# A bias table indexed by distance, read in both directions by the product, in an attention-and-MLP kernel

## The chip, the cores and the metric

The kernel runs on one core of a Trainium2 chip. The metric is the device time of one execution in microseconds (us): 1127.53 us is the median of three runs of the kernel before (1126.89 to 1128.61).

## The reference

```
q, k, v: 4 batches x 8 heads x 576 positions x 64, float32
rel   = pos[:, None] - pos[None, :]
x     = log1p(|rel|) / log1p(max(pos_i, 1))              # 576 x 576
bias  = relu(x[..., None] @ w1 + b1) @ w2                # hidden 32 -> one value per head
attn  = softmax(q @ k.T / 8 + bias[head])                # rows over 576 keys
x     = (attn @ v), heads side by side                   # 2304 x 512
x     = (h - tanh(h)) @ w_out, with h = x @ w_in         # 512 -> 2048 -> 512
out   = (silu(x @ w_gate) * (x @ w_val)) @ w_out2        # 512 -> 1536 -> 512
```

All of it is in float32. The bias is the same for all batches and depends on q and k positions alone. Since log1p(max(pos_i, 1)) is positive, it is divided out behind the relu: relu(w1 * log1p|i-j| + b1 * psi_i) @ w2 / psi_i, with psi_i = log1p(max(i, 1)).

## The kernel before

There are four stages on one core: the bias rows are made, then 80 attention units run, then the first MLP, then the second. The MLPs take most of the span and are not touched.

**Bias rows.** 576 query positions make 36 groups G of 16 positions (`GEN_ORDER`: 32 to 35, 24 to 31, 16 to 23, 8 to 15, 0 to 7). A group has four blocks j of four positions; the partitions of a block are 4 positions x 32 hidden values. `bias_hidden(G)` makes for each block a tile `r` of 576 columns (one per key): a slice of the constant table `cst` (w1 * log1p of a distance, 1152 columns wide, multiplied by w1 on the chip in two pieces, L129), plus the block's own `b1p` column, clipped at zero. Blocks 0 to 2 are made on VectorE (DVE, L144), block 3 on ScalarE (ACT, L146). `bias_rows(G)` multiplies the four tiles by w2 on TensorE into one PSUM tile `bps` (128 partitions = 16 positions x 8 heads): four products of 512 columns (L166), four of 64 (L171), each run as two passes. ACT scales them by -1/psi (`nipsi`) into the row tile `bev` (L176), GpSimd (POOL) copies 64 columns to the row's front (L180), and SP stores the tile into a scratch tensor in DRAM (L182). The hidden tiles of the next group are issued ahead of the products of this one. There are four `r` buffers of two blocks each, and five `bev` buffers.

Keys stand in a permuted order: the first 512 as (t, p) for key 4p + t, and for the odd head of a pair the last 64 in front. That is why the product writes PSUM with `"p (t n) -> p n t"` and why the row has 64 columns twice.

**Order.** Each engine runs its instructions in the order in which the code emits them, without a scheduler. 33 groups are made ahead of the first attention unit (`GEN0`, `GEN_EACH`, `GEN_LATE`), with the loads and transposes of the first head pair between them; the last three groups (letter G in `FIRST_ORDER` and `STEP_ORDER`) lie in units 0 and 1. All DMAs are issued by SP, in order, on one hardware queue; a DMA that waits holds those behind it. A DMA's completion is counted on one of eight semaphores in turn (`DMAHW0` to `DMAHW7` where an order is shown), so a ninth DMA waits for the first of them to land. `due` says after how many further groups the finished 128-position table t is loaded back from the scratch (`bias_load`, tile `bt`, L193).

**Attention.** A unit is a head pair hp, a batch b and a span t of 128 queries (t = 4, 3, 2, 1, 0; 64 for t = 4). Scores are three products into PSUM (L315), DVE adds the bias and takes the row minimum (L330), ACT exponentiates (L341), POOL scales by the inverse sum (L359), TensorE transposes the probabilities (L381, L398), and the product with v (L436) follows. For the next pair TensorE transposes q and k (L243) into a PSUM tile of the pool that the scores use too; ACT copies them out (`kraw` L259, `qraw` L254 and L262), which frees that tile.

## Time and profile before

| what | us |
|---|---|
| median of three runs | 1127.53 (1126.89 to 1128.61) |
| the profiled execution | 1127.98 |
| its span (first to last instruction) | 1126.2 |
| around the span | 1.8 |
| TensorE (PE) busy | 1106.5 (98%) |
| VectorE (DVE) busy | 863.0 (77%) |
| ScalarE (ACT) busy | 765.2 (68%) |
| GpSimd (POOL) busy | 476.9 (42%) |

The chain of waits that ended last gives 84% of the span to PE, 7% to DVE and 3% to ACT. Shares over the whole span are means over four stages. The bias rows are made in the first 57.5 us; the rows further below look into that stretch. A busy PE is not PE at its peak: a product of 32 rows that runs beside three others is counted as busy for as long as any of them runs.

### The profile page before, as it was taken

Reading aid. Unit: us, or ns where it says so; the run is one execution under the profiler, and the core shown is the slowest. Engines: PE = TensorE matmul, PEld = TensorE weight load, DVE = VectorE, ACT = ScalarE, POOL = GpSimd, SP = SyncE. Lnnn points to the kernel's source line nnn. Section 1 sums busy time; section 2 is a strip of 40 time slices with the busy share of each in tenths; the row PEclk is TensorE's granted clock in tenths of the full one; section 3 lists DMA queues with packets and bytes.
Section 4 is the critical chain, followed back from the end, with each engine's and each line's share of the span. In section 5 each row is a group of like instructions: output and inputs, shape, how many; then the busy total and the mean of one; then the engine's idle time right before and its main releaser. Section 6 shows DMA issues by size and latency. Waiting matters only on the chain.

```text
span 1126.2 us, 21423 instructions
## 1 busy us (share of the span) xinstructions
PE 1106.5 (98%) x7772; PEld 925.4 (82%) x7772; DVE 863.0 (77%) x1691; ACT 765.2 (68%) x1530; POOL 476.9 (42%) x499
## 2 busy tenths in 40 slices
PE   7999999999999999999999999999999999999998
PEld 4577777777678888888888888999999999988887
DVE  7978999999698898989988888987667765774222
ACT  7989999999588888777777786546445445443112
POOL 3357777777445365344434344124323222351000
PEclk9999999999999999999999999999999999999999
DMA  5863535351111111101100010041422422763433
GB/s 190 293 173 103 154 81 168 83 172 53 49 57 56 38 51 43 57 19 57 57 19 29 29 38 1 21 138 58 139 89 72 140 85 79 251 204 103 158 94 112
DMA packets 93034, 107.47 MB, mean 95 GB/s; under 512 B 45312, under 2 KB 72064, under 8 KB 92928
## 3 DMA queue, kind: packets, MB, share of 16 engines
q1 hardware_dynamic: 92928, 106.10, 30.1%
q8 instruction: 61, 1.00, 0.4%
q14 instruction: 45, 0.37, 0.1%
HBM read 75.41 MB, written 30.67 MB: 94 GB/s over the span
## 4 chain that ended last, share of the span: by engine, by line
PE 84%; DVE 7%; ACT 3%; issue 1%; POOL 1%; DMA 1%; DVEq 0%; ACTq 0%; POOLq 0%
PE b L720 19%; PE h L720 17%; PE y L720 16%; PE o L720 13%; PE x L436 7%; PE s L315 6%; PE pTa L381 2%; DVE acc L62 1%; PE pTb L381 1%; ACT p L341 1%; DVE r L144 1%; PE pE L398 1%; DVE p L330 1%; DMA bias<-bev 1%; DVE w L62 1%
## 5 line engine op out<-in xcount | busy, mean ns | idle before, releaser
L720 PE MATMUL y<-gh,w 128*128 128x512 f32 (+1 forms) x748 | 197.3, 369 | 1.3 <-DVE xl L451 0.9
L720 PE MATMUL h<-xh,w 128*128 128x512 f32 (+1 forms) x640 | 191.0, 369 | 0.0
L720 PEld LDWEIGHTS y<-gh,w 128*128 128x128 f32 x748 | 133.9, 188 | 26.3 <-DVE xl L451 1.4
L720 PEld LDWEIGHTS h<-xh,w 128*128 128x128 f32 x640 | 116.9, 188 | 20.7 <-issue 0.5
L359 POOL TENSOR_SCALAR p<-p,r 128x576 f32<-128x576 f32 x144 | 109.6, 773 | 49.9 <-PE s L315 15.7
L720 PE MATMUL h<-xl,w 128*128 128x512 f32 (+1 forms) x320 | 117.8, 368 | 0.0
L341 ACT ACTIVATE p<-p,m 128x576 f32<-128x576 f32 x144 | 111.2, 775 | 1.2 <-DVE m L330 0.8
L330 DVE CUSTOM_DVE_ANT_0 p<-s,bt 128x576 f32<-128x576 f32 x144 | 103.6, 753 | 10.3 <-PE s L315 10.3
L720 PE MATMUL o<-w,xh 128*128 128x512 f32 x324 | 102.7, 389 | 0.0
L720 PE MATMUL b<-xh,w 128*128 128x384 f32 x360 | 101.3, 335 | 0.5 <-DVE sq L1209 0.5
L315 PEld LDWEIGHTS s<-k,q 64*128 64x128 f32 x768 | 57.6, 184 | 28.4 <-issue 17.6
L720 PE MATMUL y<-gl,w 128*128 128x512 f32 (+1 forms) x212 | 78.8, 372 | 1.8 <-POOL gl L62 1.8
L436 PE MATMUL x<-pt,vn 128*64 128x256 f32 (+1 forms) x512 | 79.1, 421 | 0.2 <-DVE xl L451 0.2
L315 PE MATMUL s<-k,q 64*128 64x288 f32 x768 | 73.1, 310 | 0.1
L62 POOL TENSOR_TENSOR gl<-g,gh 128x512 fp32r<-128x512 f32 (+1 forms) x27 | 33.2, 1230 | 90.4 <-issue 46.3
L720 PEld LDWEIGHTS o<-w,xh 128*128 128x128 f32 x324 | 60.8, 188 | 12.4
L720 PEld LDWEIGHTS h<-xl,w 128*128 128x128 f32 x320 | 60.4, 189 | 9.9
L720 PEld LDWEIGHTS b<-xh,w 128*128 128x128 f32 x360 | 65.9, 188 | 1.0 <-ACT acc21r L1102 0.8
L720 PE MATMUL b<-xl,w 128*128 128x384 f32 x180 | 60.2, 334 | 0.0
L829 ACT ACTIVATE sq<-h 128x512 f32<-128x512 f32 (+1 forms) x40 | 22.2, 556 | 50.7 <-PE h L720 50.7
L166 PE MATMUL bps<-r,cst 128*32 128x512 f32 x264 | 48.8, 634 | 7.6 <-DVE r L144 5.7
L720 PE MATMUL o<-w,xl 128*128 128x512 f32 x144 | 56.2, 390 | 0.0
(263 smaller groups left out, 2973.8 us busy)
## 6 DMA issues: line engine op xcount, KB each, us to landing
raw_out<-in_moe_w_out_dram SPq DMA_DIRECT2D x28, 512.0 KB, 3.5
bias<-bev SPq DMA_DIRECT2D x36, 320.0 KB, 3.4
bt<-bias SPq DMA_DIRECT2D x16, 576.0 KB, 5.1
s<-sq SPq DMA_DIRECT2D x24, 384.0 KB, 3.1
raw_in<-in_moe_w_in_dram SPq DMA_DIRECT2D x16, 512.0 KB, 4.0
xh<-s SPq DMA_DIRECT2D x15, 512.0 KB, 3.6
raw_gate<-in_moe_w_gate_dram SPq DMA_DIRECT2D x12, 512.0 KB, 3.8
raw_val<-in_moe_w_val_dram SPq DMA_DIRECT2D x12, 512.0 KB, 3.8
```

What stands on the lines that cost most here:

```text
L62: (engine or nc.gpsimd).tensor_tensor(out, a, b, ALU.subtract)
L144: nc.vector.tensor_scalar(r, src, b1, 0.0, ALU.add, ALU.max)
L166: nc.tensor.matmul(ps[0][32 * j:32 * j + 32].rearrange("p (t n) -> p n t", t=4), self.w2, R[j][:, 0:512].rearrange("p (n t) -> p n t", t=4 ...
L315: nc.tensor.matmul(self.st[u][j][:, e, 0:HALF], lhs, k[r, y, e * HALF:(e + 1) * HALF], start=n == 0, stop=n == 2,)
L330: nc.vector.tensor_tensor_reduce(out=p[:, n, :].rearrange("p (e f) -> p e f", e=2), in0=ps[n][:, :, 0:HALF], in1=bt[:, n, :].rearrange("p ...
L341: nc.scalar.activation(p[:, n, :], p[:, n, :], AF.Exp, bias=m[:, n:n + 1], scale=-1.0, accum_out=ls[:, n:n + 1],)
L359: nc.gpsimd.tensor_scalar(p[:, n, :], p[:, n, :], r[:, n:n + 1], 1.0, ALU.mult, ALU.mult)
L381: nc.tensor.transpose(half[h][:, 64 * m:64 * m + 64], p[r, j, k:k + 128], self.ident[r, r])
L398: self.nc.tensor.transpose(self.pt_end[:, at:at + 128], both, self.ident)
L436: nc.tensor.matmul(ps[r, 0:n], lhs, rhs, start=c == 0, stop=c == 4)
L720: nc.tensor.matmul(out, lhs[a], rhs[b], start=first and n == 0, stop=last and n == 2, skip_group_check=again)
L829: nc.scalar.activation(u, h, AF.Square)
```

## The change

The table now holds one column per distance: 576 columns instead of 1152, and column d is w1 * log1p(d) on all partitions. Seen from the last of a group's 16 positions, column c of its row lies at distance |16G + 15 - c|, and so one clipped tile serves both sides of the diagonal: the product reads it backwards (a step of -1) up to column 16G + 15, and forwards from there. The other 15 positions need the same row, shifted by one key each; the store does that. A group clips only as many columns as its largest distance needs, n = max(16G + 16, 576 - 16G), between 304 and 576. In ten groups (odd G from 9 to 27) DVE makes all four blocks, in the others three. The product of a group now has three segments of four (cut at column 16G + 15, where the direction turns, and at 512, where the PSUM bank ends), 591 columns in all instead of 576. The row tile has 591 columns; the store writes it into DRAM with a row pitch that is one element longer per position (`H * ROW + 1`), which shifts each position to its place. The POOL copy is gone. Keys stand in natural order; the odd head's bias is loaded back in two pieces, so a `bt` load is three DMAs instead of one (or two); v is loaded with two DMAs of 256-byte pieces; k is transposed like q, and `kraw` is copied in two instructions. The tables are loaded back six groups after they are due instead of two.

The table comes in with one DMA per 32 partitions, and in the last 32 partitions two columns are then overwritten by two small DMAs.

```diff
@@ -35,6 +35,8 @@
 C_W1 = C_NIPSI + NBLK
 C_B1, C_W2 = C_W1 + 1, C_W1 + 2
 NCONST = C_W2 + QG * H
+K_PSI, K_W1, K_B1, K_W2 = (c - TABW + S for c in (C_PSI, C_W1, C_B1, C_W2))
+ROW, BASE, WIDE = 640, 16, S + 15
 
 
 TORDER = (4, 3, 2, 1, 0)
@@ -102,18 +104,20 @@
         c = self.gen_p
         self.ident = self.const.tile([128, 128], F32, name="ident")
         make_identity(nc, self.ident)
-        self.cst = c.tile([128, NCONST], F32, name="cst")
-        nc.sync.dma_start(out=self.cst[:, TABW:NCONST], in_=self.packed[:, TABW:NCONST])
-        half = 640
-        nc.sync.dma_start(out=self.cst[:, 0:half], in_=self.packed[:, 0:half])
-        nc.sync.dma_start(out=self.cst[:, half:TABW], in_=self.packed[:, half:TABW])
-        b1c = self.cst[:, C_B1:C_B1 + 1]
+        self.cst = c.tile([128, S + NCONST - TABW], F32, name="cst")
+        nc.sync.dma_start(out=self.cst[:, S:], in_=self.packed[:, TABW:NCONST])
+        for g in range(QG):
+            at, x = slice(HID * g, HID * g + HID), S - 1 + g
+            nc.sync.dma_start(out=self.cst[at, 0:S], in_=self.packed[at, x:x + S])
+        for d in (S - 2, S - 1):
+            x = S - 1 + QG - 1 - d
+            nc.sync.dma_start(out=self.cst[at, d:d + 1], in_=self.packed[at, x:x + 1])
+        b1c = self.cst[:, K_B1:K_B1 + 1]
         self.b1p = c.tile([128, NBLK], F32, name="b1p")
-        nc.vector.tensor_scalar(self.b1p, self.cst[:, C_PSI:C_PSI + NBLK], b1c, None, ALU.mult)
-        self.table(self.cst[:, 0:half])
-        self.rest = self.cst[:, half:TABW]
-
-        self.w2 = self.cst[:, C_W2:NCONST]
+        nc.vector.tensor_scalar(self.b1p, self.cst[:, K_PSI:K_PSI + NBLK], b1c, None, ALU.mult)
+        t = self.cst[:, 0:S]
+        nc.vector.tensor_scalar(t, t, self.cst[:, K_W1:K_W1 + 1], None, ALU.mult)
+        self.w2 = self.cst[:, K_W2:]
         self.nipsi = c.tile([128, NG], F32, name="nipsi")
         rows = self.packed.rearrange("(g r) c -> g r c", g=QG)
         blocks = c.tile([128, NBLK], F32, name="blocks")
@@ -122,25 +126,19 @@
             nc.sync.dma_start(out=blocks[at, :], in_=rows[:, 0:H, C_NIPSI:C_NIPSI + NBLK])
             nc.gpsimd.tensor_copy(self.nipsi[at, :], blocks[at, j::4])
 
-        self.scratch = [self.dram.tile([n * H, S + 64], F32, name=f"bias_{t}") for t, (_, n) in enumerate(SPANS)]
-
-    def table(self, t):
-
-        self.nc.vector.tensor_scalar(t, t, self.cst[:, C_W1:C_W1 + 1], None, ALU.mult)
+        self.scratch = [self.dram.tile([n, H, ROW], F32, name=f"bias_{t}") for t, (_, n) in enumerate(SPANS)]
 
     def bias_hidden(self, G):
 
         nc = self.nc
         both = [self.gen_p.tile([128, 2, S], F32, tag="r", name=f"r_{G}_{i}", bufs=4) for i in range(2)]
         self.R[G] = []
-        if G == GEN_ORDER[1]:
-            self.table(self.rest)
         for j in range(4):
             blk = 4 * G + j
-            o = S - 1 - QG * blk
-            r = both[j // 2][:, j % 2, :]
-            src, b1 = self.cst[:, o:o + S], self.b1p[:, blk:blk + 1]
-            if j < 3:
+            n = max(16 * G + 16, S - 16 * G)
+            r = both[j // 2][:, j % 2, 0:n]
+            src, b1 = self.cst[:, 0:n], self.b1p[:, blk:blk + 1]
+            if j < 3 or 8 <= G < 28 and G % 2:
                 nc.vector.tensor_scalar(r, src, b1, 0.0, ALU.add, ALU.max)
             else:
                 nc.scalar.activation(r, src, AF.Relu, bias=b1, scale=1.0)
@@ -162,24 +160,27 @@
             both = None
             ps = [self.bank(tag, f"bps{tag}_{G}") for tag in ("cx" if n % 2 else "ab")]
 
-        for j in range(4):
-            nc.tensor.matmul(
-                ps[0][32 * j:32 * j + 32].rearrange("p (t n) -> p n t", t=4), self.w2,
-                R[j][:, 0:512].rearrange("p (n t) -> p n t", t=4), start=True, stop=True,
-            )
-        for j in range(4):
-            nc.tensor.matmul(ps[1][32 * j:32 * j + 32, 0:64], self.w2, R[j][:, 512:S], start=True, stop=True)
-        row = self.gen_p.tile([128, S + 64], F32, tag="bev", name=f"bev_{G}", bufs=BEV_BUFS)
-        out = row[:, 64:S + 64]
+        zero = 16 * G + 15
+        cuts = sorted({0, zero, 512, WIDE})
+        for a, b in zip(cuts, cuts[1:]):
+            d = a - zero
+            for j in range(4):
+                moving = R[j][:, d:d + b - a] if d >= 0 else R[j][:, -d:-d - (b - a):-1]
+                nc.tensor.matmul(
+                    ps[a // 512][32 * j:32 * j + 32, a % 512:a % 512 + b - a], self.w2, moving, start=True, stop=True,
+                )
+        row = self.gen_p.tile([128, WIDE], F32, tag="bev", name=f"bev_{G}", bufs=BEV_BUFS)
+        out = row
         ni = self.nipsi[:, G:G + 1]
         if both is not None:
-            nc.scalar.activation(out, both.rearrange("p e n -> p (e n)")[:, 0:S], AF.Copy, scale=ni)
+            nc.scalar.activation(out, both.rearrange("p e n -> p (e n)")[:, 0:WIDE], AF.Copy, scale=ni)
         else:
             nc.scalar.activation(out[:, 0:512], ps[0], AF.Copy, scale=ni)
-            nc.scalar.activation(out[:, 512:S], ps[1][:, 0:64], AF.Copy, scale=ni)
-        nc.gpsimd.tensor_copy(row[:, 0:64], row[:, S:S + 64])
+            nc.scalar.activation(out[:, 512:WIDE], ps[1][:, 0:WIDE - 512], AF.Copy, scale=ni)
         t, r0 = divmod(G, 8)
-        nc.sync.dma_start(out=self.scratch[t][128 * r0:128 * r0 + 128, :], in_=row)
+        to = self.scratch[t][16 * r0:16 * r0 + 16]
+        at = bass.AP(to.tensor, to.offset + BASE - 15, [[H * ROW + 1, 16], [ROW, H], [1, WIDE]])
+        nc.sync.dma_start(out=at, in_=row)
 
     def bias_load(self, hp, t):
         n = SPANS[t][1]
@@ -187,13 +188,14 @@
             [128, n // 64, S], F32, tag=f"bias{n}", name=f"bt_{hp}_{t}", bufs=4 if n == 128 else 1,
         )
 
-        x = 2 * hp * (S + 64) + 64
-        src = self.scratch[t].rearrange("(q h) k -> q (h k)", h=H)[:, x:x + 2 * S]
-        if n == 128:
-            self.nc.sync.dma_start(out=bt.rearrange("p j k -> p (j k)"), in_=src)
-        else:
-            for j in range(2):
-                self.nc.sync.dma_start(out=bt[64 * j:64 * j + 64, 0, :], in_=src[:, j * S:j * S + S])
+        for j in range(2):
+            src = self.scratch[t][:, 2 * hp + j, BASE:BASE + S]
+            to = bt[:, j] if n == 128 else bt[64 * j:64 * j + 64, 0]
+            if j == 0:
+                self.nc.sync.dma_start(out=to, in_=src)
+            else:
+                self.nc.sync.dma_start(out=to[:, 64:S], in_=src[:, 0:512])
+                self.nc.sync.dma_start(out=to[:, 0:64], in_=src[:, 512:S])
         self.bias_t[hp, t] = bt
 
 
@@ -203,9 +205,8 @@
         a = {"q": self.q, "k": self.k, "v": self.v}[nm][b, 2 * hp:2 * hp + 2]
         if nm == "v":
             t = self.nat.tile([128, 2, 4, D], F32, tag="v", name=f"vn_{hp}_{b}", bufs=2)
-            nc.sync.dma_start(
-                out=t.rearrange("p j t d -> p j (t d)"), in_=a[:, 0:512].rearrange("j (p t) d -> p j (t d)", t=4),
-            )
+            for j in range(2):
+                nc.sync.dma_start(out=t[:, j], in_=a[j, 0:512].rearrange("(t p) d -> p t d", t=4))
 
             end = self.vend[self.nbuf["v"] % 2]
             self.nbuf["v"] += 1
@@ -225,16 +226,16 @@
         t = self.nt[hp, b, "k"]
         nc.sync.dma_start(out=t[:, 0:4, 0, :], in_=by4(0, 0, 512))
         nc.sync.dma_start(out=t[0:64, 4, 0, :], in_=a[0, 512:576])
-        nc.sync.dma_start(out=t[0:64, 0, 1, :], in_=a[1, 512:576])
-        nc.sync.dma_start(out=t[64:128, 0:4, 1, :], in_=by4(1, 0, 256))
-        nc.sync.dma_start(out=t[0:64, 1:5, 1, :], in_=by4(1, 256, 512))
+        nc.sync.dma_start(out=t[0:16, 0:4, 1, :], in_=by4(1, 512, 576))
+        nc.sync.dma_start(out=t[16:128, 0:4, 1, :], in_=by4(1, 0, 448))
+        nc.sync.dma_start(out=t[0:64, 4, 1, :], in_=a[1, 448:512])
 
     def qk_transpose(self, hp, b, which):
 
         nc = self.nc
         nat = self.nt.pop((hp, b, which))
         ps = self.ps_s.tile([128, 2, 512], F32, tag="s", name=f"{which}T_{hp}_{b}")
-        parts = [(slice(t, 256, 4) if which == "q" else slice(64 * t, 64 * t + 64), nat[:, t, :, :]) for t in range(4)]
+        parts = [(slice(t, 256, 4), nat[:, t, :, :]) for t in range(4)]
         if which == "k":
             parts.append((slice(256, 320), nat[:, 4, :, :]))
         for to, a in parts:
@@ -255,12 +256,11 @@
                 self.qraw[:, 0:512].rearrange("p (h n) -> p h n", h=2), ps[:, :, 0:256], AF.Copy, scale=-0.125,
             )
             return
-        kraw = self.shared.tile([128, 640], F32, tag="one1", name=f"kraw_{hp}_{b}")
-        nc.scalar.copy(
-            kraw.rearrange("p (t h n) -> p t h n", t=5, h=2), ps[:, :, 0:320].rearrange("p h (t n) -> p t h n", t=5),
-        )
+        kraw = self.shared.tile([128, S], F32, tag="one1", name=f"kraw_{hp}_{b}")
+        nc.scalar.copy(kraw[:, 0:512].rearrange("p (h n) -> p h n", h=2), ps[:, :, 0:256])
+        nc.scalar.copy(kraw[:, 512:S], ps[:, 0, 256:320])
         nc.scalar.activation(self.qraw[:, 512:S], ps[:, 1, 256:320], AF.Copy, scale=-0.125)
-        self.raw_qk += [(hp, b, "q", self.qraw), (hp, b, "k", kraw[:, 0:S])]
+        self.raw_qk += [(hp, b, "q", self.qraw), (hp, b, "k", kraw)]
 
     def qk_high(self):
         nc = self.nc
@@ -487,7 +487,7 @@
                     self.bias_rows(G)
                     done = NG - len(gens)
                     if not any(x // 8 == G // 8 for x in gens):
-                        due.append((G // 8, done + 2))
+                        due.append((G // 8, done + 6))
                     if due and done >= due[0][1]:
                         self.bias_load(0, due.pop(0)[0])
                     if not gens:
```

On SP's queue the program now starts as follows (`cst` is the table, `blocks` the factors for the rows, `qn` and `kn` the first pair's q and k, `bev` the first row). Before:

```order
L106 DMA cst<-in_packed_dram 128x322
L108 DMA cst<-in_packed_dram 128x640
L109 DMA cst<-in_packed_dram 128x512
L122 DMA blocks<-in_packed_dram 32x1x144 x4
L222 DMA qn_0_136<-in_q_dram 128x4x64
L222 DMA qn_0_136<-in_q_dram 128x4x64 [waits DMAHW0_49]
```

and in the changed kernel:

```order
L108 DMA cst<-in_packed_dram 128x322
L111 DMA cst<-in_packed_dram 32x576 x4
L114 DMA cst<-in_packed_dram 32x1 [waits DMAHW4_49]
L114 DMA cst<-in_packed_dram 32x1
L126 DMA blocks<-in_packed_dram 32x1x144
L126 DMA blocks<-in_packed_dram 32x1x144 [waits DMAHW0_49]
```

The first small DMA waits for the fourth table DMA (semaphore 4), whose columns it overwrites, and everything behind it on SP waits with it.

On DVE and PE one group in the middle, G = 20 (the 17th that is made), read before:

```order
L144 TENSOR_SCALAR r_0_520<-cst,b1p 128x576 x2
L144 TENSOR_SCALAR r_1_521<-cst,b1p 128x576
L166 MATMUL bps_545<-r_0_520,cst 32x128x4 x2
L166 MATMUL bps_545<-r_1_521,cst 32x128x4 x2
L171 MATMUL bps_545<-r_0_520,cst 32x64 x2
L171 MATMUL bps_545<-r_1_521,cst 32x64 x2
```

and G = 20 and the clipping of G = 21 read now:

```order
L142 TENSOR_SCALAR r_0_526<-cst,b1p 128x336 x2
L142 TENSOR_SCALAR r_1_527<-cst,b1p 128x336
L142 TENSOR_SCALAR r_0_548<-cst,b1p 128x352 x2
L142 TENSOR_SCALAR r_1_549<-cst,b1p 128x352 x2
L169 MATMUL bps_554<-r_0_526,cst 32x335 x2
L169 MATMUL bps_554<-r_1_527,cst 32x335 x2
L169 MATMUL bps_554<-r_0_526,cst 32x177 x2
L169 MATMUL bps_554<-r_1_527,cst 32x177 x2
L169 MATMUL bps_554<-r_0_526,cst 32x79 x2
L169 MATMUL bps_554<-r_1_527,cst 32x79 x2
```

Each clipping instruction is narrower, the odd group has a fourth one on DVE, and the products are in three segments instead of two.

## Rows read from the trace of the kernel before

**Rows 1.** Windows by stretch: busy us and (instructions) of PE, PEld, DVE, ACT, POOL; PEclk; DMA share; GB/s.

```profile
20.00:30.00 10.00, 9.68 (x108) 4.25 (x108) 9.46 (x23) 9.94 (x17) 2.66 (x6) 1.00 0.60 219
30.00:40.00 10.00, 10.00 (x122) 5.57 (x115) 9.93 (x23) 9.99 (x16) 4.05 (x8) 1.00 0.90 305
...
50.00:57.50 7.50, 5.91 (x62) 2.60 (x60) 5.19 (x12) 6.65 (x10) 2.02 (x5) 1.00 0.98 302
140.00:160.00 20.00, 20.00 (x262) 14.54 (x260) 18.32 (x57) 18.66 (x48) 15.45 (x19) 1.00 0.32 85
```

**Rows 2.** Timeline from 30 us: start, us, engine, line, operation, count; merged rows.

```profile
30.85 20.29 DVE L144 TENSOR_SCALAR r<-cst,b1p 128x576 f32<-128x576 f32 x45
...
31.61 0.76 ACT L146 ACTIVATE r<-cst,b1p 128x576 f32<-128x576 f32 x1
...
32.28 0.73 ACT L176 ACTIVATE bev<-bps,nipsi 128x576 f32<-128x576 f32 x1
...
32.91 0.76 ACT L146 ACTIVATE r<-cst,b1p 128x576 f32<-128x576 f32 x1
```

**Rows 3.** Timeline from 49.5 us: the end of the stage; idle time and releaser in brackets.

```profile
50.84 0.74 ACT L176 ACTIVATE bev<-bps,nipsi 128x576 f32<-128x576 f32 x1 [2.27 <-DMA bias<-bev]
...
53.42 4.08 DVE L144 TENSOR_SCALAR r<-cst,b1p 128x576 f32<-128x576 f32 x9 [2.29 <-PE bps L171]
...
58.77 1.06 PE L166 MATMUL bpsc<-r,cst 128*32 128x512 f32 x8
...
59.65 0.29 PE L171 MATMUL bpsx<-r,cst 128*32 128x64 f32 x8
```

**Rows 4.** Timeline from 0 us: the start of the program.

```profile
0.74 0.39 SPq L106 DMA_DIRECT2D cst<-in_packed_dram  x1
...
3.12 0.29 DVE L112 TENSOR_SCALAR b1p<-cst 128x144 f32<-128x144 f32 x1 [2.20 <-DMA cst<-in_packed_dram]
...
5.11 1.38 DVE L144 TENSOR_SCALAR r<-cst,b1p 128x576 f32<-128x576 f32 x3
...
10.42 3.16 SPq L182 DMA_DIRECT2D bias<-bev  x3
```

**Rows 5.** Groups by form, 0 to 260 us: count, busy us, mean ns, idle before.

```profile
L254 ACT ACTIVATE qraw<-qT 128x512 f32<-128x512 f32 x15 | 8.9, 597 | 5.1 <-PE qT L243 5.1
...
L243 PE MATMUL kT<-ident,kn 64*128 64x64 f32 x150 | 7.5, 227 | 1.1 <-DVE m L330 1.1
...
L243 PE MATMUL qT<-ident,qn 64*128 64x64 f32 x120 | 6.9, 235 | 0.0
...
L262 ACT ACTIVATE qraw<-kT 128x64 f32<-128x64 f32 x15 | 3.7, 246 | 0.0
...
L129 DVE TENSOR_SCALAR cst<-cst 128x640 f32<-128x640 f32 x1 | 0.6, 552 | 1.1 <-DMA cst<-in_packed_dram 1.1
...
L129 DVE TENSOR_SCALAR cst<-cst 128x512 f32<-128x512 f32 x1 | 0.5, 482 | 0.0
...
L112 DVE TENSOR_SCALAR b1p<-cst 128x144 f32<-128x144 f32 x1 | 0.3, 294 | 2.2 <-DMA cst<-in_packed_dram 2.2
```

**Rows 6.** DMA queue, 14 to 16 us: packets, MB, time as a share of 16 engines.

```profile
q1 hardware_dynamic: 260, 0.62, 82.3%
```

**Rows 7.** The same from 33 to 35 us, while a table is loaded back.

```profile
q1 hardware_dynamic: 98, 0.45, 93.2%
```

**Rows 8.** The same from 3 to 4 us, while the constant table comes in.

```profile
q1 hardware_dynamic: 174, 0.37, 96.3%
```

**Rows 9.** Timeline from 163 us: the middle of an attention pair.

```profile
163.82 0.60 PE L436 MATMUL x<-pe,vend 128*64 128x256 f32 x4
...
164.12 0.23 ACT L262 ACTIVATE qraw<-kT 128x64 f32<-128x64 f32 x1
...
164.36 0.93 PE L315 MATMUL s<-k,q 64*128 64x288 f32 x9
```

**Rows 10.** Timeline from 61 us: the last table's load and its first use.

```profile
67.47 0.32 SPq L193 DMA_DIRECT2D bt<-bias  x1
...
72.22 0.76 DVE L330 CUSTOM_DVE_ANT_0 p<-s,bt 128x576 f32<-128x576 f32 x1
```

## The prediction

> **What bounds the kernel now.** I read the windows first, then the timeline of the stretch that the change touches, then the waits in it. From 57.5 us on PE carries the program: from 140 to 160 us it is busy 20.00 of 20 us, with DMA at 0.32 [rows 1]. The edits there add no columns to PE, so it is the bias stage ahead of it, 57.5 us long, in which time can be won. There PE is also shown busy, but DVE and ACT set the pace: from 30 to 40 us they are busy 9.93 and 9.99 of 10 us [rows 1]. 45 clippings on DVE start in 20.29 us, 0.451 us each, so three of a group take 1.35 us. ACT's clip and eviction start 0.67 us apart and the next clip 0.63 us later, 1.30 us for a group [rows 2]. PE could go faster: eight passes of 512 columns start in 0.88 us (58.77 to 59.65) where their tiles had long been ready [rows 3], so a group of 576 columns needs about 0.99 us. A third limit comes late in the stage: DMA is at 0.98 from 50 to 57.5 us [rows 1], ACT waits 2.27 us for a row buffer whose store hasn't landed, and DVE idles 2.29 us behind it [rows 3].
>
> **Fewer columns to clip.** A clipping's slope comes from the same kind of instruction at two widths: 552 ns at 640 columns, 294 ns at 144 [rows 5], 0.52 ns for a column; at 576 one costs 0.451 us [rows 2]. The stage clips for 34 groups (33 that it makes, and the next one's). Before, DVE spends 34 x 1.353 = 46.0 us there. With n columns and three or four clippings a group, DVE takes 5.3 us for groups 32 to 35, 10.1 for 24 to 31, 9.1 for 16 to 23, 9.9 for 8 to 15 and 7.7 for 0 to 5: 42.2 us. That is 3.8 less, and the table's second multiplication goes too, 0.48 us [rows 5]: 4.3 us off DVE. ACT's slope is 0.78 ns a column (597 ns at 512, 246 at 64 [rows 5]; both read PSUM, so for a clip it is an estimate). Before, ACT spends 34 x 1.30 = 44.2 us. Ten of its clips go (10 x 0.63 = 6.3 us), the other 24 are shorter by some 2.5 us, and 15 more evicted columns cost 34 x 0.012 = 0.4: about 8 us off. ACT no longer paces the whole stage, and where it still has extra work, copying the first heads (20 to 30 us: ACT 9.94, DVE 9.46 [rows 1]), the half microsecond that DVE lost for it comes back. DVE with three and four clippings in turn and ACT with one clip or none won't mesh perfectly. I take 4.4 us, between 2.5 and 5.0.
>
> **The product.** 591 columns at 0.88 us for 512 are 1.02 us a group, and there are 24 passes instead of 16. DVE's smallest mean is 9.1 / 8 = 1.14 us a group, so PE stays behind DVE, and this edit costs nothing as long as a column read backwards takes what one read forwards does. No row shows a backward read; that is a rival below.
>
> **The table's start: a wait added.** Before, the first load is issued at 0.74 us and its data is used at 3.12, 2.4 us later; the first clipping starts at 5.11 [rows 4]. Now four table loads follow at about 0.45 us each, the last at 2.55, landing at about 4.95. The first small load waits for that, the second follows at 5.4, and after another 2.4 us the table is complete at 7.8. One multiplication of 576 columns, 0.52 us, and the first clipping starts at 8.3 us: 3.2 us later. It shifts the whole stage, since nothing runs beside it. Bounds: 2.4 us (one landing more and the rest hidden) and 4.8 (two landings more). Behind the small loads on SP stand the row factors and the first q and k loads, and then the row stores: the first store moves from 10.42 us [rows 4] to about 14.3. Five row buffers take the first five groups meanwhile, some 8 us from 11.9 on, so nobody waits for it.
>
> **The stall at the end of the stage.** A store's packet of 2560 bytes takes 0.823 x 32 / 260 = 0.101 us of an engine [rows 6], so a store takes 8 x 0.101 = 0.81 us of all sixteen; 2364 bytes at that rate are 0.75. While a table is loaded back in packets of 4608 bytes, a packet takes 0.932 x 32 / 98 = 0.30 us, stores among them [rows 7]; the constant table's loads of 2560 and 2048 bytes took 0.963 x 16 / 174 = 0.089 [rows 8]. A table in pieces of 2304 bytes and less should therefore occupy the engines for about 1.3 us instead of 2.4 or more, and with its later due time the fourth table leaves the stage. The rows also go to SP without the copy on POOL. On the other side the groups come faster. Of the 2.3 us I take half, 1.2 us won; bounds 0 and 2.3.
>
> **The attention units.** `kraw` becomes two copies; 512 columns take 597 ns and 64 take 246, and instructions on ACT overlap by about 0.1 us [rows 2, 5], so the tile that the next scores need comes free some 0.1 us later, once a pair. PE's product before those scores ends at 164.42 us and ACT's last copy at 164.35 [rows 9]: the slack is 0.07 us, and what is late next is PE. Fifteen pairs at 0.04 us give 0.6 us; bounds 0 and 15 x 0.14 = 2.1 us (the whole second copy). The last table is issued at 67.47 and used at 72.22 us [rows 10], with no idle time to spare; its store now goes out without the copy ahead of it, which covers the two further issues. The loads of v take 512 more small packets a pair, on queues at a share of 0.32 [rows 1]: nothing. k's transposes now write PSUM with a step of four, as q's do: 235 instead of 227 ns [rows 5], overlapped, nothing.
>
> The same rows bear on a rule. The Trainium skill says in "SBUF — State Buffer", section "Door 1: The DMA port swizzle", that PSUM has lines of 8 bytes and that "any non-contiguous PSUM access pattern significantly slows down matmuls". By that rule k's transposes would be dearer; at the difference of q's and k's means it would be 16 x 10 x 8 ns = 1.3 us at most. The trace doesn't bear it out for the bias product, whose strided writes of 512 columns start 0.11 us apart with four tiles running side by side [rows 3]. The same section gives SBUF lines of 16 bytes, at full rate while accesses stay in a line; by it a step of -1 in float32 is as fast as +1, which no row here shows.
>
> **Sum.** -4.4 (clipping) + 3.2 (start) - 1.2 (stall) + 0.6 (attention) = -1.8 us, and about -0.5 for the three groups made beside units 0 and 1, whose clippings shrink too by up to 0.06 us each on both engines: -2.3. Against the profiled execution's 1127.98 us (1126.2 span and 1.8 around it) that is 1125.7; the median of the runs lies 0.45 lower, so I predict 1125.2 us. 0.2% (2.3 us) is about what a measurement here can tell from no change; the forecast lies on that edge. With all bounds together: -5.0 - 2.3 + 2.4 - 0.5 = -5.4, and -2.5 + 4.8 + 2.1 = +4.4, so 1122.1 to 1131.9.
>
> **Rivals.**
> 1. The gain meets the start and nothing is left: the engines mesh badly (2.5 us) and the stall stays because groups come faster. -2.5 + 3.2 + 0.6 - 0.5 = +0.8: 1128.3 us. For it: the stage's DMA is at 0.9 or more from 30 us on. Against: fewer bytes, shorter packets.
> 2. Slower: stores become the bound. Each packet now starts at an address that is shifted by 4 bytes a position. From the first store at 14.3 us to the end of the stage at about 54 there are some 40 us for 33 stores and two and a half tables (3.3 us); with more than 36.7 / 33 / 8 = 0.139 us a packet (0.101 now), stores decide. At 0.16 us the stores take 42.2 us, and with the tables the stage ends at 59.8 instead of 57.5: +2.3 + 0.6 - 0.5 gives 1129.9 us, small loads not counted.
> 3. Slower: a backward column takes twice a forward one. Then a group takes 1.02 x (1 + (16G + 15) / 591): about 2.0 us for groups 32 to 35, 1.8 for 24 to 31, 1.6 for 16 to 23 and 1.4 for 8 to 15, all above DVE. The sum is 8 + 14.4 + 12.7 + 11 + 6.5 = 52.6 us, as long as the stage was with its stall, and the later start isn't paid for: +3.2 + 0.6 = 1131.3 us. It decides from a price of about 1.2 on.
>
> **Chances.** The forecast, with its terms at their means give or take, 0.63: 1122.8 to 1127.5, of which 0.38 lies below 1125.3. Rival 1: 0.16, nearly all within 0.2%. Rival 2: 0.08. Rival 3: 0.07. More than my best bound, or a cost that I haven't seen in the attention units: 0.03 on either side. Faster by over 0.2%: 0.38 + 0.03 = 0.41. Slower: 0.08 + 0.07 + 0.03 + 0.02 of rival 1 = 0.20. Same: 0.39. The range, 1122.6 to 1131.0, leaves out about 0.06 below and 0.12 above.
>
> **What would show it.** Start: first clipping at 8.3 us, two small loads at 5.0 and 5.4. Clipping: DVE's instructions 0.31 to 0.45 us apart with no idle time in groups 16 to 23, and ACT idle there. Product: its passes of 335 and 177 columns at 1.7 ns a column for four side by side, in both directions. Stores: packets of 2364 bytes at 0.095 us; no wait of ACT for a row buffer. Stage: the first scores' product at about 55.5 us instead of 57.4. Attention: distances between pairs equal to within 0.1 us. It is wrong if the first scores start later than before.

## The result, and the profile after the change

The changed kernel takes 1137.24 us, median of 6 runs (1134.63 to 1143.51), the one before 1127.63 (6 runs, 1126.89 to 1128.61): 1.0092 times as long by all runs together, 95% interval 1.0063 to 1.0120. Forecast were 1125.2 us, 1122.6 to 1131.0. The profiled execution of the changed kernel is the longest of its six, 1143.51 us (span 1141.4), so its trace shows more loss than the median. The two runs above 1140 us have a mean granted TensorE clock of 0.996, the other four of 0.998 to 1.000.

The same piece of work, looked up in both timelines, shows where the time went:

| start of | before | after | later by |
|---|---|---|---|
| the first clipping | 5.11 | 7.08 | 2.0 |
| the 23rd group's eviction | 41.77 | 42.57 | 0.8 |
| the 33rd group's eviction | 57.55 | 62.23 | 4.7 |
| the second unit's bias addition | 62.79 | 66.59 | 3.8 |
| unit 5's bias addition (pair 2) | 78.02 | 85.48 | 7.5 |
| a unit early in the third head pair | 186.08 | 197.01 | 10.9 |
| a unit early in the fourth head pair | 244.84 | 259.50 | 14.7 |
| end of the span | 1126.2 | 1141.4 | 15.2 |

Inside the units, between these places, the shift stays the same within 0.15 us. So there are four losses: the start, the end of the bias stage, unit 5, and a step at two changes of the head pair. Two stretches win: the clipping up to the 23rd group, 1.2 us, and the way from the 33rd group to the second unit, with the last three groups, 0.9.

Windows of the changed kernel, with the columns of [rows 1]:

```profile
20.00:30.00 10.00, 9.71 (x173) 4.58 (x172) 8.58 (x25) 9.30 (x19) 0.00 (x0) 1.00 0.68 192
30.00:40.00 10.00, 9.79 (x187) 7.14 (x183) 9.49 (x28) 7.45 (x14) 0.00 (x0) 1.00 0.89 245
40.00:50.00 10.00, 9.05 (x168) 6.23 (x167) 8.57 (x25) 5.92 (x9) 0.00 (x0) 1.00 0.91 268
78.00:82.00 4.00, 2.19 (x40) 1.75 (x38) 2.32 (x9) 1.59 (x4) 1.91 (x3) 0.95 0.44 99
82.00:86.00 4.00, 4.00 (x38) 3.71 (x40) 0.52 (x1) 2.54 (x9) 2.71 (x4) 0.63 0.41 91
186.00:190.00 4.00, 1.87 (x33) 1.59 (x30) 2.25 (x5) 2.78 (x10) 3.48 (x5) 1.00 1.02 359
190.00:194.00 4.00, 4.00 (x36) 2.88 (x36) 2.69 (x8) 2.19 (x5) 1.85 (x3) 0.60 0.64 155
```

From 40 to 50 us no engine is full any more. At 78 and at 186 us PE idles about half of 4 us, and in the 4 us behind that it is granted 0.63 and 0.60 of its clock: mostly the 1.2 GHz level. That nearly doubles what a wait of some 2 us costs: 1.8 us idle and 4 x 0.37 = 1.5 us of clock at unit 5, 2.1 and 4 x 0.40 = 1.6 at the third head pair, where the shifts grow by 3.7 and 3.5.

The start, from the timeline (against [rows 4]): the first small load is issued at 4.55 us, the table is multiplied at 6.53, so a small load lands in some 1.5 us (2.4 were forecast), and the first store goes out at 13.72 instead of 10.42.

```profile
4.55 0.78 SPq L114 DMA_DIRECT2D cst<-in_packed_dram  x2
6.53 0.52 DVE L119 TENSOR_SCALAR cst<-cst 128x576 f32<-128x576 f32 x1 [2.94 <-DMA cst<-in_packed_dram]
7.08 2.54 DVE L142 TENSOR_SCALAR r<-cst,b1p 128x528 f32<-128x528 f32 x6
```

The pace in the middle, ACT's timeline (against [rows 2]): evictions at 34.86, 37.39 and 39.98, every second one, lie 2.53 and 2.59 us apart; before it was 2.70.

```profile
34.86 0.75 ACT L176 ACTIVATE bev<-bps,nipsi 128x591 f32<-128x591 f32 x1 [0.64 <-PE bps L169]
35.52 0.59 ACT L144 ACTIVATE r<-cst,b1p 128x368 f32<-128x368 f32 x1
36.01 0.75 ACT L176 ACTIVATE bev<-bps,nipsi 128x591 f32<-128x591 f32 x1
37.39 0.76 ACT L176 ACTIVATE bev<-bps,nipsi 128x591 f32<-128x591 f32 x1 [0.64 <-PE bps L169]
38.04 0.66 ACT L144 ACTIVATE r<-cst,b1p 128x448 f32<-128x448 f32 x1
38.60 0.74 ACT L176 ACTIVATE bev<-bps,nipsi 128x591 f32<-128x591 f32 x1
39.98 0.75 ACT L176 ACTIVATE bev<-bps,nipsi 128x591 f32<-128x591 f32 x1 [0.64 <-PE bps L169]
```

The stores, DMA queue from 24 to 26 us (packets, MB, share of 16 engines, as in [rows 6]); before:

```profile
q1 hardware_dynamic: 137, 0.31, 40.5%
```

and after:

```profile
q1 hardware_dynamic: 207, 0.45, 82.4%
```

0.405 x 32 / 137 is 0.095 us for a packet, 0.824 x 32 / 207 is 0.127. These are means over all packets of the window, and 16 of each count are packets of 4 bytes. By the trace's records of single packets, from 12 to 75 us, a store's packet of 2560 bytes took 0.106 us before, and one of 2364 bytes takes 0.125 now: smaller and nearly a fifth dearer. Two thirds of these take 0.09 to 0.10; a quarter take more than 0.14.

The end of the stage (against [rows 3]): from 49.45 to 56.25 us SP issues five loads of k and three pieces of a table, with one store among them, and the eviction at 60.98 waits 2.91 us for a row buffer. Between 20 and 66 us ACT waits 6.4 us for row buffers in 5 waits; before, 2.3 us in one.

```profile
53.35 0.55 SPq L183 DMA_DIRECT2D bias<-bev  x1
53.94 1.33 SPq L195 DMA_DIRECT2D bt<-bias  x1
55.31 0.46 SPq L197 DMA_DIRECT2D bt<-bias  x1
55.82 0.43 SPq L198 DMA_DIRECT2D bt<-bias  x1
56.35 9.04 SPq L183 DMA_DIRECT2D bias<-bev  x8
60.98 0.75 ACT L176 ACTIVATE bev<-bps,nipsi 128x591 f32<-128x591 f32 x1 [2.91 <-DMA bias<-bev]
```

Unit 5 (against [rows 10], where the last table is issued at 67.47 us): it goes out at 72.48, the loads of pair 2 behind it. The second load of q lands at 78.96, PE's transposes of q start at 79.09, and DVE idles 4.08 us until the unit's scores come. (`fill` are products whose result isn't used.)

```profile
72.48 0.33 SPq L195 DMA_DIRECT2D bt<-bias  x1
72.86 0.43 SPq L197 DMA_DIRECT2D bt<-bias  x1
73.33 0.43 SPq L198 DMA_DIRECT2D bt<-bias  x1
73.86 1.28 SPq L223 DMA_DIRECT2D qn<-in_q_dram  x2
...
79.31 0.62 SPq L231 DMA_DIRECT2D kn<-in_k_dram  x1
...
81.29 0.69 PE L244 MATMUL kT<-ident,kn 64*128 64x64 f32 x10 [1.23 <-DVE r L350]
81.90 2.07 PE L404 MATMUL fill<-ident 128*128 128x128 f32 x8
...
85.48 0.76 DVE L330 CUSTOM_DVE_ANT_0 p<-s,bt 128x576 f32<-128x576 f32 x1 [4.08 <-PE s L315]
```

The third head pair: a weight load stands behind three pieces of a table and ahead of nine more. It lands after 5.8 us; DVE waits 1.72 us for it with the work that PE needs next (L451) behind it in its queue.

```profile
180.46 0.54 SPq L195 DMA_DIRECT2D bt<-bias  x1
181.05 0.51 SPq L197 DMA_DIRECT2D bt<-bias  x1
181.62 0.42 SPq L198 DMA_DIRECT2D bt<-bias  x1
182.14 0.38 SPq L620 DMA_DIRECT2D raw_out<-in_moe_w_out_dram  x1
...
186.41 1.47 POOL L359 TENSOR_SCALAR p<-p,r 128x576 f32<-128x576 f32 x2 [0.93 <-PE x L436]
...
187.92 1.40 POOL L64 TENSOR_TENSOR q<-qraw,q 128x576 fp32r<-128x576 f32 x1
187.93 1.67 DVE L661 TENSOR_SCALAR bits_out<-raw_out 128x512 int32<-128x512 int32 x1 [1.72 <-DMA raw_out<-in_moe_w_out_dram]
189.52 0.41 DVE L451 TENSOR_TENSOR xl<-x,xh 128x256 fp32r<-128x256 f32 x1
...
189.99 1.66 PE L436 MATMUL x<-pt,vn 128*64 128x320 f32 x8 [2.13 <-DVE xl L451]
```

The late instruction L661 also takes 1.67 us: it has slipped from beside POOL's L359 to beside POOL's L64, an operation on two tensors. Before, the same instruction takes 0.405 (count, min/median/max in ns, first and last start):

```profile
L661 DVE TENSOR_SCALAR bits_out<-raw_out x2: 405/405/405, 178.8 to 237.5; 128x512 int32<-128x512 int32 x2
```

### The profile page after: what moved, and what is told of

Read it like the earlier page. It is cut to its first block, busy times and chain, and to the rows that moved or that the text cites. A ratio compares the mean times of both kernels' runs of the same rounds, so it can differ in the third digit from the quotient of the medians.

```text
span 1141.4 us, 22052 instructions
## 1 busy us (share of the span) xinstructions
PE 1110.0 (97%) x8060; PEld 933.2 (82%) x8060; DVE 860.5 (75%) x1700; ACT 757.1 (66%) x1536; POOL 458.9 (40%) x463
## 4 chain that ended last, share of the span: by engine, by line
PE 82%; DVE 8%; ACT 4%; DMA 2%; issue 1%; POOL 1%; SPq 1%; DVEq 0%; ACTq 0%; POOLq 0%
PE b L720 18%; PE h L720 17%; PE y L720 16%; PE o L720 13%; PE x L436 7%; PE s L315 5%; PE bps L169 2%; PE pTa L381 1%; DVE p L330 1%; DVE acc L64 1%; DMA bias<-bev 1%; ACT p L341 1%; PE pTb L381 1%; DMA bt<-bias 1%; PE pE L398 1%
## 5 line engine op out<-in xcount | busy, mean ns | idle before, releaser
L359 POOL TENSOR_SCALAR p<-p,r 128x576 f32<-128x576 f32 x144 | 109.2, 769 | 117.7 <-ACT bev L178 57.7
L64 POOL TENSOR_TENSOR gl<-g,gh 128x512 fp32r<-128x512 f32 (+1 forms) x27 | 32.9, 1218 | 91.3 <-issue 46.9
L169 PE MATMUL bps<-r,cst 128*32 128x79 f32 (+38 forms) x792 | 47.1, 349 | 11.6 <-DVE r L142 7.8
```

The costliest lines, as they stand in the source:

```text
L64: (engine or nc.gpsimd).tensor_tensor(out, a, b, ALU.subtract)
L169: nc.tensor.matmul(ps[a // 512][32 * j:32 * j + 32, a % 512:a % 512 + b - a], self.w2, moving, start=True, stop=True,)
L359: nc.gpsimd.tensor_scalar(p[:, n, :], p[:, n, :], r[:, n:n + 1], 1.0, ALU.mult, ALU.mult)
```

## The experiments

Given are the median and the ratio to the kernel before, measured beside it, with its 95% interval; the ratio is over all runs and so not quite that of the medians. "Back" is the difference from the changed kernel's median, 1137.24. Runs of the changed kernel and of its variants spread over 2 to 9 us, so a difference below 2 us between two of them is not read. Each run has one profile, of one execution. The diffs are shortened; `...` marks what is left out.

### The suspects one by one, and together

`e1_start`:

```diff
-            nc.sync.dma_start(out=self.cst[at, 0:S], in_=self.packed[at, x:x + S])
-        for d in (S - 2, S - 1): ...
+            nc.sync.dma_start(out=self.cst[at, 0:S], in_=self.packed[0:HID, S - 1:2 * S - 1])
```

> All four table loads read the first 32 rows from distance 0, and the two small loads behind them are gone. The multiplication of the table then waits for the fourth table load alone, so the first clipping should start at about 5.6 us instead of 7.08 (before: 5.11). Theory (three separate losses: the stage, the late loads of pair 2, the two changes of the head pair): the stage starts 1.5 us earlier, and its row stores with it, so about 1.5 us of the 9.6 us come back: 1135.7 us. Rival (the stage is bound by its stores from the middle on, and a start earlier by 1.5 us only makes it wait longer there): 0, 1137.2 us.

1137.91 us, 1.0105 [1.0077, 1.0133]. The first clipping starts at 5.37, the 33rd eviction 0.8 us earlier than in the changed kernel: half of what was won is waited away at the stage's end, and the whole time doesn't fall, as the rival said. Mended alone, the start gives nothing back that these runs can tell.

`e2_bt_v_one`:

```diff
-        for j in range(2): ... three dma_start of bt[:, j] pieces
+            self.nc.sync.dma_start(out=bt, in_=self.scratch[t][:, 2 * hp:2 * hp + 2, BASE:BASE + S])
...
-                nc.sync.dma_start(out=t[:, j], in_=a[j, 0:512].rearrange("(t p) d -> p t d", t=4))
+            nc.sync.dma_start(out=t..., in_=a[:, 0:512].rearrange("j (p t) d -> p j (t d)", t=4))
```

> Tables are read back in one DMA each (as before the change) and v in one DMA of 1 KB pieces a pair; the rest as in the changed kernel. The bias of the odd head is left in unrotated key order and v's keys are permuted, so only the time is to be read. Theory (SP issues more DMAs than it can in time: 9 more a head pair for tables and 1 a pair for v): at the starts of the third and fourth head pair nothing is late any more, 2 x 3.6 us back, and of the 3.6 us at unit 5 the part that bt_0's two further issues cost, about 1.3: 7.2 + 1.3 = 8.5, 1128.7 us. Rival (the stores of the stage cost it all, the later losses follow from the stage's lateness): 0 to 1 us back, 1136.5 or more. Rival (backward reads): 0.

1132.16 us, 1.0043 [1.0028, 1.0058]: 5.1 back, where the theory said 8.5. Both steps at the head pairs are gone from its trace (the shift stays at 3.5 to 3.7 us from unit 5 to the fourth head pair).

`e3_aligned`:

```diff
-        at = bass.AP(to.tensor, to.offset + BASE - 15, [[H * ROW + 1, 16], [ROW, H], [1, WIDE]])
+        at = bass.AP(to.tensor, to.offset + BASE, [[H * ROW, 16], [ROW, H], [1, WIDE]])
```

> Every row of a group is stored at the same 64-byte address step, without the shift of 4 bytes a position; the bias then stands at wrong distances, so only the time is to be read. Theory: a packet of 2364 bytes takes 0.089 us instead of 0.123 to 0.127 in the stage, ACT's wait for row buffers (6.4 us in 5 waits) shrinks to under 3, and the first scores come about 2 us earlier: 1135.3 us; if pair 2's loads also get out of the way of bt_0 it is 3.6 more, 1131.7. The two losses of 3.6 us at the third and fourth head pair stay. Rival (size, not alignment, sets the packet's time): packets still at 0.12 us, 1137.2 us.

1135.56 us, 1.0072 [1.0057, 1.0087]: 1.7 back. From 24 to 26 us the queue shows

```profile
q1 hardware_dynamic: 208, 0.42, 54.0%
```

0.083 us a packet against 0.127, with 31 packets of 4 bytes among the 208; of the 2364-byte packets alone, from 12 to 75 us, 0.100 against 0.125. The address of the write, not its size, makes it dear. The stage doesn't follow: ACT waits 7.7 us for row buffers instead of 6.4, 4.2 of them ahead of the 32nd eviction in a stretch with DMA at 1.00 (55.6 to 60 us), and the 33rd eviction stands at 62.45, no earlier than in the changed kernel. The whole time is as the theory said, but not by its way.

`e4_all_four` (e1, e2 and e3 together):

> The three edits together (start without the small loads, tables and v in one DMA each, stores without the shift); bias and v in wrong places, so only the time is to be read. Theory: the losses are separate and all come from these three, so the sum 1.5 + 8.5 + 2.0 to 5.6 is 12 to 15 us: 1122 to 1125 us, below the kernel before, since what is left of the change is the shorter clipping. Rival (a part of the loss lies in the product's backward reads or in the units): 1128 us or more.

1128.99 us over 10 runs, 1.0007 [0.9998, 1.0017]: 8.2 back, but not below before, as the theory had it. A loss was left: the 23rd eviction stood 1.0 us ahead of before, the 33rd 1.1 behind.

### Tables or v, and the pieces alone

`e14_v_one` and `e15_bt_one` are the two halves of e2:

> The changed kernel with v read in one DMA of 1 KB pieces a pair as before the change (v's keys are permuted, so only the time is to be read). Theory (the tables' pieces are what delays the transfers behind them): 0 to 1 us back, 1136 to 1137 us. Rival (v's 1024 packets of 256 bytes a pair ahead of the tables and of the weight load at the head pairs): 3 us or more back, 1134 us or less.

> The changed kernel with each table read back in one DMA as before the change (the odd head's bias is left in unrotated key order, so only the time is to be read). Theory (nine further issues a head pair on SP, two of them ahead of pair 2's loads and of a weight load): 4 to 5 us back, 1132 to 1133 us. Rival (v's packets): 1 us or less.

v in one DMA: 1139.10 us, 1.0098 [1.0080, 1.0116], nothing back. Tables in one DMA: 1133.57, 1.0056 [1.0043, 1.0069], 3.7 back (4 to 5 were expected), and no step at the head pairs. It is the tables' pieces that count, not v's.

`e8_before_pieces` does both to the kernel before:

```diff
-            self.nc.sync.dma_start(out=bt.rearrange("p j k -> p (j k)"), in_=src)
+            for x, y in ((0, S),) if j == 0 else ((64, S), (0, 64)):
+                self.nc.sync.dma_start(out=to[:, x:y], in_=src[:, j * S + x:j * S + y])
```

> The kernel before the change, with one thing of it alone: tables read back in three DMAs each instead of one, and v in two DMAs of 256-byte pieces a pair instead of one of 1 KB pieces (v's keys then stand in another order, so only the time is to be read). Theory (SP's queue is full at the changes of the head pair and before pair 2): 1 to 1.5 us lost at unit 5, and 0.7 to 3.6 us at each of the third and fourth head pair: 1130 to 1136 us. Rival (these losses come only with the later stage and the shifted stores): 1128 us.

1128.92 us, 1.0008 [0.9998, 1.0017]: 0.8 us more, 2 us at most by the interval, and not the 2 to 8 that the theory gave. Its profile is of its slowest run (1131.15) and shows losses at the same places: 1.6 us at the end of the stage, 1.0 at unit 5, 0.7 at the third head pair. So the pieces cost little where nothing else is late; the theory of a queue that is too long by itself is too simple. That the costs collide is what fits: no run takes the collision apart.

### The weight load

`e17_defer`:

```diff
-                    self.bias_load(hp + 1, t)
+                    later.append((hp + 1, t))
...
                 aside(last - i)
+            while later:
+                self.bias_load(*later.pop())
```

> In the attention units, the reading back of a next head pair's table is issued at the end of a step instead of in its middle, so that the weight load for the second part, which DVE waits for at the third and fourth head pair, stands ahead of the three pieces of a table on SP instead of behind them. Everything is computed as in the reference. Theory (the weight load lands after 5.8 us behind the pieces, DVE waits 1.7 us for it and its next instruction then runs beside POOL's for 1.6 us instead of 0.4): it lands 2 us or more earlier, the steps at the third and fourth head pair are gone from every run: median 1134.5 us, none above 1136.5. Rival (the many packets, not the order, delay it): as the changed kernel, 1137 us with single runs above 1140.

1135.07 us, 1.0079 [1.0065, 1.0093], but two of five runs at 1138: the bound of 1136.5 was missed. In its trace the load lands after 3.8 us, and the instruction that had waited takes 0.406 us both times (count, min/median/max in ns, first and last start):

```profile
L663 DVE TENSOR_SCALAR bits_out<-raw_out x2: 405/406/406, 184.2 to 243.3; 128x512 int32<-128x512 int32 x2
```

against, in the changed kernel,

```profile
L661 DVE TENSOR_SCALAR bits_out<-raw_out x2: 1552/1609/1666, 187.9 to 250.4; 128x512 int32<-128x512 int32 x2
```

The late weight load makes the steps of the profiled execution. One profile without a step would not show that, for the steps vary: 12 kernels here were profiled with three pieces of a table ahead of the load (the changed kernel, e1, e3, e5, e6, e7, e8, e9, e12, e13, e14, e18), 24 places in all. At six of them DVE waits 1.7 to 2.2 us for the load, the instruction behind takes 1.2 to 1.7 us, the granted clock falls to its lower level right after, and the step is 3.5 to 4.9 us. At twelve DVE waits 1.0 to 1.7, the instruction takes 0.9 at most, the clock stays up, and the step is 0.7 to 0.9. At the other six DVE waits 0.9 at most and there is no step. With tables in one DMA (before, e2, e4, e10, e15), or the load ahead of the pieces (e17), DVE never waits for it, and the step is 0 to 0.2.

The two longer runs of e17 left no trace; their mean granted clock is 0.998 and 0.997, that of the other three 1.000, so in them too PE stood still long enough somewhere to lose clock. Where, stays open. Over all its runs e17 is not clear of the changed kernel: 2.2 us between the medians, with overlapping runs.

### When the tables are read

`e7_due2` (`done + 6` becomes `done + 2`), `e10_all_four_due2` (the same with e4), and `e12_pool_tables` (`dma = self.nc.sync if hp else self.nc.gpsimd`):

> The tables are read back two groups after their last group instead of six, as before the change. Theory (the late tables put bt_1 and bt_0 ahead of pair 2's loads): bt_0 is issued at about 68.5 instead of 72.48, pair 2's queries and keys follow some 4 us earlier, and the 3.6 us at unit 5 are gone; against it the loads of 4.6 KB a row come while rows are stored, ACT waits for row buffers 1 to 2 us more: 1134 to 1136 us. Rival (the later reading back saves more in the stage than it costs at unit 5): 1138 us or more.

> The four edits of the start, the tables, v and the stores together (bias and v in wrong places, so only the time is to be read), and the tables read back two groups after their last group instead of six. With the four edits alone the rows were 1.0 us ahead of before up to the 23rd group and 1.1 us behind after the 33rd. Theory (the late tables meet the loads of queries and keys between 40 and 51 us, and the stores wait behind both): the wait for row buffers falls to the 2.3 us that it was before, the stage ends 1 to 2 us earlier than before, 1126 to 1127.5 us. Rival (the same transfers in a shorter time, whatever their order): 1129 us, and the stage's end as with six.

> The tables of the first head pair are read back from POOL's queue, which is idle in the stage, instead of SP's; nothing else changes. Theory (SP's queue, in order: in 16.6 us from 39.8 on it spends 11 us in issues that aren't row stores): ACT's waits for row buffers fall from 6 us to 3 or less, and pair 2's loads no longer stand behind bt_0, so unit 5 loses 1.3 us less: 1132 to 1135 us. Rival (the DMA engines' own time is the bound, share 0.9): the same waits, 1136 to 1138 us.

e7: 1137.91 us, 1.0073 [1.0048, 1.0098]; unit 5 loses 1.1 us instead of 3.6, but the first scores come 3.1 us later than in the changed kernel (62.32 against 59.25): no change, as the rival said. e10: 1127.65 us, 0.9998 [0.9989, 1.0008], all of the loss gone; ACT's waits for row buffers are down to 1.6 us, the 33rd eviction stands at 56.76 (before 57.55), and everything after it 0.9 to 1.0 earlier. e10 and e4 differ by this edit alone, ten runs each, with intervals that just overlap. So the late reading costs at most where stores and pieces leave time for the early one; in the mended kernels below it changes nothing that can be read (e16 against e11). e12: 1139.99 us, 1.0110 [1.0095, 1.0125], 2.8 us slower than the changed kernel, which neither side had foreseen: POOL waits 44 us in its queue for the stores of whole tables, and the units' work on it stands behind. In the stage it speaks for the rival: with the tables' issues off SP, ACT's waits stayed at 6.2 us, so it is not the issues of tables on SP that make ACT wait.

### The pace of the clipping

`e5_forward` (`R[j][:, 0:b - a]` in place of the backward read), `e6_two` (the row starts at PSUM column `512 - zero`, two segments instead of three), `e13_r5` (`bufs=5`), `e18_double` (the list of segments `* 2` for groups 16 to 23):

> The columns left of distance 0 are read forwards too (from distance 0 on) instead of backwards; all passes, widths and addresses written stay as they are, so the bias of these columns is in the wrong order and only the time is to be read. In the changed kernel two groups in the middle of the stage (groups 16 to 23) take 2.56 us, before 2.70, predicted 2.28, and the chain of waits runs over PE's product there. Theory (number of passes: 24 of a group instead of 16, the short ones at 0.23 us whatever their width): the two groups still take 2.56 us, the whole time is unchanged at 1137 us, give or take 2. Rival (a column read backwards costs more): the two groups fall to 2.4 us or less, and the stage's middle is shorter by 0.08 us or more a group; whole time down by 1 to 3 us.

> For groups 4 to 31 the row of a group begins in PSUM at such a column that distance 0 falls on the border between the two banks: the product then has two segments (16 passes of a group) instead of three (24), and the eviction reads the same 591 columns from there. Theory (number of passes sets PE's pace in the middle): two groups there take 2.3 to 2.45 us instead of 2.56, DVE's seven clippings being the bound then, and groups 31 to 4 end some 2 us earlier as far as the row stores allow it; the first bias addition 0.5 to 2 us earlier, 1135 to 1136.5 us. Rival (DVE and ACT mesh badly, PE only waits for them): still 2.56 us, 1137.2 us. The losses at the head pairs stay.

> The clipped tables have five tiles (of two blocks each) instead of four, so that DVE can clip half a group further ahead of the product. Theory (DVE waits for a tile that the product still reads, 0.15 to 0.26 us every two groups): two groups in the middle take 2.35 us instead of 2.53, and the 23rd eviction comes about 1.5 us earlier (41.0 us instead of 42.57); after it the row stores take most of it back: 1136 to 1137 us. Rival (the clippings' own pace, or ACT's chain from eviction to eviction, is the bound): 2.5 us, the 23rd eviction as before within 0.3 us.

> The product of groups 16 to 23 is made twice, into the same place; nothing else changes. Two groups take 2.53 us there. Theory A (PE's product paces them: 1.27 us a group): twice that, 5.0 us for two groups. Theory B (PE alone needs 1.0 us a group, and the pace comes from the chain clipping, product, eviction, next clipping): 4.1 to 4.3 us for two groups. Whole time 8 to 12 us more than the changed kernel in either case.

1138.16 us, 1.0087 [1.0072, 1.0102]; 1134.89, 1.0061 [1.0046, 1.0077]; 1136.79, 1.0086 [1.0069, 1.0103]; 1140.29 in one run. In e5, e6 and e13 two groups still take 2.5 to 2.6 us: the direction, a third of the passes and a tile more change nothing of the pace. (e6's median is 2.3 us lower for all that; its runs overlap with the changed kernel's, and no cause shows.) That a backward column costs what a forward one does is seen in the passes themselves. One of 367 columns runs backwards in the changed kernel and forwards in e5 (count, busy us, mean ns):

```profile
L169 PE MATMUL bps<-r,cst 128*32 128x367 f32 x8 | 1.7, 484 | 0.0
```

and this line is the same, word for word, in both.

In e18 a doubled product takes 2.01 us (evictions at 34.44, 36.45, 38.46):

```profile
34.44 0.76 ACT L176 ACTIVATE bev<-bps,nipsi 128x591 f32<-128x591 f32 x1 [1.28 <-PE bps L169]
...
36.45 0.75 ACT L176 ACTIVATE bev<-bps,nipsi 128x591 f32<-128x591 f32 x1 [0.79 <-PE bps L169]
38.46 0.75 ACT L176 ACTIVATE bev<-bps,nipsi 128x591 f32<-128x591 f32 x1 [1.26 <-PE bps L169]
```

so a single one needs 1.0 us, less than the 1.27 that a group takes: PE's product is not what paces the groups (theory B's 4.0 us for two groups, not theory A's 5.0). In the rows of the middle above, a chain closes over ACT: the eviction from 37.39, 0.65 us later the clipping of the next even group, 0.66, and 1.28 from its end to that group's eviction, 2.59 us for two groups. This last is read from the trace; no run took ACT's clipping out. DVE's own seven clippings lie close below: they start 0.32 to 0.37 us apart, 2.3 to 2.5 us for two groups, so DVE is not ruled out as the bound.

### Mended kernels that compute everything

`e9_shift_load` (stores aligned, each partition's source at the read 4 bytes less far), `e11_best` (that, with e1, e6, a table in two DMAs and k in four), `e16_best_due2` (that, and `done + 2`):

```diff
+        at = bass.AP(to.tensor, to.offset + LEAD - 16 * r0, [[H * ROW, 16], [ROW, H], [1, WIDE]])
...
+            src = bass.AP(src.tensor, src.offset, [[H * ROW - 1, n], [ROW, 2], [1, S]])
```

> The rows of a group are stored at 64-byte aligned addresses, and the shift of 4 bytes a position is made where a table is read back (each partition's source starts 4 bytes less far); everything is computed as in the reference. Theory (a write to unaligned addresses costs more, a read from them doesn't): the stage as with aligned stores alone, packets of a store at 0.09 us, tables landing as before (3.7 us median), 1135.5 us. Rival (reads from unaligned addresses cost a quarter more too): the tables take 0.3 us longer each, in the stage and at the head pairs, 1137 us or more.

> Everything is computed as in the reference: the start without the two small loads, two segments of the product for groups 4 to 31, aligned stores with the shift at the read, a table read back in two DMAs instead of three (columns 0 to 511 of both heads, then 512 to 575 of both, which lie side by side in the tile), and k in four DMAs instead of five. Theory (number of issues on SP and unaligned writes are the loss): near the four edits together, with one DMA more a table and a pair: 1129 to 1131 us. Rival (unaligned reads or the small packets cost it): 1133 us or more.

> Everything is computed as in the reference: the start without the two small loads, two segments of the product for groups 4 to 31, aligned stores with the shift at the read, tables in two DMAs each, k in four, and the tables read back two groups after their last group. Theory (early tables take the collision out of the stage's end): 2 to 3 us below the same kernel with six groups (1131.2): 1128 to 1129 us, about the time before the change. Rival (what is left is small packets and DMAs on SP in the units, not the stage): 1131 us.

1137.24 us, 1.0076 [1.0057, 1.0094]; 1131.18, 1.0027 [1.0018, 1.0037]; 1130.27, 1.0022 [1.0011, 1.0033]. In e9 a store's packet of 2364 bytes takes 0.100 us, as in e3, so the shift is cheap to store that way; but nothing comes back. The 2304-byte pieces of a table land 4.2 us (median) after their issue instead of 3.7, the 2048-byte ones 4.1 instead of 4.2, so an unaligned read is not shown to be dearer. e11 and e16 win back 6 to 7 us and stay behind the kernel before; e16's 2 to 3 us over e11, and with them the time before, were not reached.

## Why the prediction was wrong

The sign that it had named came: the first scores start later than before, at 59.25 us instead of 57.38. By its own terms:

| term | forecast | measured in the profiled execution |
|---|---|---|
| start | +3.2 (2.4 to 4.8) | +2.0; mended alone it gives nothing back in the whole (e1) |
| clipping | -4.4 (-2.5 to -5.0) | -1.2 by the 23rd group; in e10, with no loss at the start, the 30th eviction is 2.0 ahead of before |
| stall at the stage's end | -1.2 (0 to -2.3) | +3.9 (23rd to 33rd eviction: 19.66 against 15.78 us) |
| three late groups | -0.5 | -0.9 (33rd eviction to second unit) |
| units | +0.6 (0 to 2.1) | 0.1 for `kraw`'s copy over 14 pairs (e10); +3.6 at unit 5, 3.5 and 3.7 at two changes of the head pair |

**Right:** the product. 1.02 us a group was forecast and 1.0 measured, and backward columns cost what forward ones do (e5's passes); the rival on them falls. v's small packets cost nothing that shows (e14). k's transposes with a step of four take 223 ns (median, 60 to 260 us), as they did without it.

**Wrong in size, the clipping.** The step "DVE's smallest mean is 9.1 / 8 = 1.14 us a group" took DVE's own instructions for the pace. They do start 0.32 to 0.37 us apart; but two groups take 2.5 to 2.6 us, as the chain over ACT and PE does, and of 0.42 us forecast for two groups 0.11 to 0.17 remain. Which of the two bounds, a close one of DVE's or ACT's chain, is not settled.

**Wrong in sign, the stall.** "2364 bytes at that rate are 0.75": the rate was taken from aligned rows (and from a mean with 4-byte packets in it; the store's own were 0.106, not 0.101), and a shifted store needs 8 x 0.125 = 1.0 us. That was the second rival's mechanism, below the 0.139 us from which it was to decide, so I gave it 0.08. A table in pieces was to take 1.3 us of the engines; by its packets it takes 128 x (0.126 + 0.094 + 0.018) / 16 = 1.9, before 128 x 0.304 / 16 = 2.4. Where loads of q and k and a table come between, 1.0 us of DMA in 1.27 leaves little room, and the later due time, counted as a gain, put a table just there. No one of the three is shown to be the cause by itself: against 62.23 us in the changed kernel, the 33rd eviction stands at 62.45 with aligned stores (e3), at 62.46 with the early reading (e7), at 61.01 with whole tables (e15); with all of them and the start mended (e10) at 56.76.

**Wrong, and the largest: "its store now goes out without the copy ahead of it, which covers the two further issues".** The two further issues of a table were weighed at bt_0 alone and cost 3.7 us of the 9.6 (e15). A cost in the units that I hadn't seen had a chance of 0.03. At unit 5 they stand, with the late stage, ahead of pair 2's loads. At the head pairs nobody was looked for behind them on SP: the weight load is there, behind it DVE, behind DVE PE. I had listed queues for the stage and not for the places, 120 us later, where the same function issues the same DMAs.

What made it worse than each cost: PE's clock. A wait of some 2 us on PE is followed by 4 us at 0.60 to 0.63; in e14's profile, where PE idles 0.7 to 1.2 us at the same places, the granted clock stays at 1.00. The steps and unit 5's loss are those of the longest execution: at unit 5 the other profiles with pieces and shifted stores show 1.1 to 2.5 us (e12, whose first tables don't go through SP, aside). Not settled: why the pieces alone cost 0.8 us in the kernel before (e8) and 3.7 here; that they meet later stores and a later stage is argued, and e10 fits it, but no run separates the pair.
